# Decoding 64-bit weights: magnitudes on VectorE, signs as 16-bit floats, and three weight loads behind copies of keys and scores

## The chip, the core and the metric

The kernel runs on one core of one Trainium2 chip. The metric is the device time of one execution in microseconds (us); shorter is better. The engines are TensorE (PE: matmuls and transposes; PEld: its weight loads), VectorE (DVE), ScalarE (ACT), GpSimd (POOL) and SyncE (SP, which here issues DMAs). Each works through its own list of instructions in order; semaphores join the lists.

## The reference

Attention over the 32 largest scores of each row, then a feed-forward block with an ELU between two products. Cut to what matters:

```python
# q, k, v: (8, 8, 576, 64) float32
scores = (q @ k.transpose(0, 1, 3, 2)) / sqrt(64)
kth    = the 32nd largest score of each row
attn   = softmax of the scores >= kth (all others -1e9)
x      = (attn @ v), heads side by side      # (4608, 512)
# w_in (512, 2048) and w_out (2048, 512) arrive as float64
h = x @ w_in
g = where(h > 0, h, exp(min(h, 0)) - 1)
out = g @ w_out                              # (4608, 512) float32
```

## The kernel before

**Weights.** The two weight matrices arrive as 64-bit floats, and no engine computes with these. So the kernel reads them as pairs of 32-bit words and makes 32-bit floats of them itself: 16 tiles of `w_in` and 16 of `w_out`, each of 128 partitions x 512 weights (512 KB as loaded). `load_weight(i)` issues the DMA of tile i into a buffer named `raw` (seven buffers). Then come, for each tile:

- `convert_first`: ScalarE makes the low word into a float whose bits hold the upper mantissa part (L174), writes the sign as an 8-bit float into the top byte of the low word's place (L175, Sign), and takes the absolute value of the high word, read as a 32-bit float (L178, Abs). GpSimd clamps that value (L179).
- `convert_last`: VectorE shifts the clamped word left by 3 (L186), and GpSimd adds the two words as integers into the final `w_in` or `w_out` tile (L187).

All these operations step over 8 bytes from one element to the next, since the high and low words alternate.

**The list of pieces.** `decode` holds 35 pieces; `hook()` takes the next one. Piece i issues the load of tile i+3, does `convert_first(i)` and then `convert_last(i-3)`. Hooks stand in VectorE's selection of the 32 largest scores: behind two of the MAX8 passes of each of the two rows' halves in steps 0 to 7, and behind three of step 8. Three loads (tiles 0 to 2) are issued ahead of all, between the loads of the first queries, keys and values.

**Steps.** A step is one block of 128 queries for a pair of heads. TensorE turns queries and keys by transposes (`transpose_qk`, copied by ScalarE into `kqT`, L264 and L277) and computes scores (L301), ScalarE copies them scaled into `sc` (L309). VectorE finds the 32 largest of each row: four MAX8 passes (L320 and L330 in `select_row` up to step 7; L343 and L355 in `select` from step 8) with three MATCH_REPLACE8 between (L324, L348). GpSimd makes two small operands (L368, L370), ScalarE masks and exponentiates (L371, L372), GpSimd normalises (L382 to L389), TensorE transposes the result (L408, copied at L409) and multiplies by the values (L434, copied at L461).

**Feed-forward.** `ffn_pieces` cuts the feed-forward work into pieces that `feed` spreads between the steps: `hidden` (L506, with ScalarE's two Relus at L516 and L519, the Exp at L521, and VectorE's joining operation at L478) and `project` (L531, output copied by ScalarE at L540, stored by SP). A piece of the first block only goes in when enough weight tiles are decoded.

**Order.** From step 8 on, and for the first keys and scores, the order of each compute engine is the written one (`manual_schedule`). In between, steps 0 to 7, the framework orders the instructions of each engine itself.

Of the kernel before, what the change touches and what calls it, by code (L numbers as in the profile page):

```python
# [8 lines left out]
AF = mybir.ActivationFunctionType  # L9
ALU = mybir.AluOpType  # L10
FP32 = mybir.dt.float32
U32 = mybir.dt.uint32
I32 = mybir.dt.int32
FP8 = mybir.dt.float8e4
PSUM = bass.MemoryType.PSUM

TOP_K = 32
# [2 lines left out]
STEEP = 1.0e30  # L20
HIDDEN = {1: 1.1, 2: 1.85, 3: 2.7}
PROJECT = 3.55


class Tile:
# [56 lines left out]
def kernel(  # L82
# [9 lines left out]
    nc = tc.nc  # L92
# [9 lines left out]
    NF = dff // P  # L102
# [3 lines left out]
    scale = 1.0 / float(D) ** 0.5  # L106
# [33 lines left out]
    raw = {}  # L140

    def weight(i):
        per = dff // WN
        if i < NC * per:
            f, c = divmod(i, NC)
            src = moe_w_in[c * P : (c + 1) * P, 2 * f * WN : 2 * (f + 1) * WN]
            return src, w_in[:, c, f * WN : (f + 1) * WN]
        f = i - NC * per
        return moe_w_out[f * P : (f + 1) * P, :], w_out[:, f, :]

    def load_weight(i):
        t = rawpool.tile([P, 2 * WN], U32, tag="raw", name="raw")
        nc.sync.dma_start(t[:], weight(i)[0])
        raw[i] = t

    def parts(t):
        words = t[:].rearrange("p (n w) -> p n w", w=2)
        signs = t[:].bitcast(FP8).rearrange("p (n w) -> p n w", w=8)
        return words[:, :, 0], words[:, :, 1], signs[:, :, 3]

    def convert_first(i):

        lo, hi, sign = parts(raw[i])
        ef, mf = hi.bitcast(FP32), lo.bitcast(FP32)
        nc.scalar.activation(mf, lo, AF.Copy, scale=2.0**-35, bias=2.0**17)  # L174
        nc.scalar.activation(  # L175
            sign, ef, AF.Sign, scale=2.0**64, bias=1.0, saturate=False
        )
        nc.scalar.activation(ef, ef, AF.Abs, scale=2.0**-62)  # L178
        nc.gpsimd.tensor_scalar(  # L179
            ef, ef, (2.0 - 2.0**-3 - 2.0**-23) * 2.0**-46, 2.0**-77, ALU.min, ALU.max  # L180
        )

    def convert_last(i):
# [21 lines left out]
    def decode_piece(i):  # L205
        if i < 2 * NF:
            if i + 3 < 2 * NF:
                load_weight(i + 3)
            convert_first(i)
        if i > 2:  # L210
            convert_last(i - 3)
            decoded[0] = i - 2

    loaded, kqT, vT = {}, {}, {}

    def load_qk(b, hp, other=nc.sync):

        for name, src in (("k", k), ("q", q)):
            n, queue = (J + 1, nc.sync) if name == "k" else (J, other)
            t = ldpool.tile([P, n, 2, D], FP32, tag=name + "in", name=name + "in")  # L220
            if name == "k":
                last = t
            for hh in range(2):
                queue.dma_start(
                    t[:, 0:J, hh, :],
                    src[b, 2 * hp + hh, 0:JP, :].rearrange("(p j) d -> p j d", j=J),
                )
            queue.dma_start(
                last[0:R, J, :, :] if name == "k" else last[R:P, J, :, :],
                src[b, 2 * hp : 2 * hp + 2, JP:S, :].rearrange("h p d -> p h d"),  # L230
            )
            loaded[b, hp, name] = t

    def load_v(b, hp):

        t = kvpool.tile([P, 2 * J + 2, D], FP32, tag="vT", name="vT")
        for hh in range(2):
            h = 2 * hp + hh
            nc.sync.dma_start(
                t[:, hh * J : (hh + 1) * J, :],  # L240
                v[b, h, 0:JP, :].rearrange("(p j) d -> p j d", j=J),
            )
            mine = slice(hh * R, (hh + 1) * R)
            other = slice((1 - hh) * R, (2 - hh) * R)
            nc.gpsimd.memset(t[other, 2 * J + hh, :], 0.0)
            nc.sync.dma_start(t[mine, 2 * J + hh, :], v[b, h, JP:S, :])
        vT[b, hp] = t
# [234 lines left out]
    def ffn_pieces(blk):  # L482
        n_tok = blk.slots * P
        bank = dm // n_tok
        unit = max(2, bank)

        def hidden(f):
            if f == 0 and blk.number == 0:
                g = early.tile([P, NF, P], FP32, tag="g", name="gT")
                blk.gT = [g[:, 0:NG], g[:, NG:NF]]  # L490
            elif f % NG == 0 and blk.number > 0:
                g = late["g"].tile([P, NG, T], FP32, tag="g", name="gT")
                blk.gT.append(g[:])
            if f % unit == 0:
                if len(gates) > 1:
                    close_gates(upto=gates[0][1])
                if blk.number == 0:
                    n = earlyf.tile([P, 4 * P], FP32, tag="n", name="n")
                else:
                    n = late["f"].tile([P, 2 * T], FP32, tag="n", name="n")  # L500
                blk.n = n[:, 0 : unit * n_tok].rearrange("p (f t) -> p f t", f=unit)
            if f % bank == 0:
                ps = ps_f.tile([P, dm], FP32, tag="f", name="hps")
                blk.h = ps[:, 0 : bank * n_tok].rearrange("p (f t) -> p f t", f=bank)
            for i in range(NC):
                nc.tensor.matmul(  # L506
                    blk.h[:, f % bank, :],
                    w_in[:, i, f * P : (f + 1) * P],
                    blk.xT[:, i, 0:n_tok],
                    start=(i == 0),  # L510
                    stop=(i == NC - 1),
                )
            g, end = blk.gT[f // NG], f % NG + 1
            if end % bank == 0:
                n0 = f % unit + 1 - bank
                nc.scalar.activation(  # L516
                    blk.n[:, n0 : n0 + bank, :], blk.h, AF.Relu, scale=-1.0
                )
                nc.scalar.activation(g[:, end - bank : end, 0:n_tok], blk.h, AF.Relu)  # L519
            if end % unit == 0:  # L520
                nc.scalar.activation(blk.n, blk.n, AF.Exp, scale=-1.0)  # L521
                dst = g[:, end - unit : end, 0:n_tok]
                gates.append((place[0], (blk.number, f + 1 - unit), dst, blk.n))

        def project(s, part):
            close_gates(upto=(blk.number, (part + 1) * NF // 4 - 1))
            if part == 0:
                blk.o = ps_f.tile([P, dm], FP32, tag="f", name="ops")
            step = NF // 4
            for f in range(part * step, (part + 1) * step):  # L530
                nc.tensor.matmul(  # L531
                    blk.o[:],
                    blk.gT[f // NG][:, f % NG, s * P : (s + 1) * P],
                    w_out[:, f, :],
                    start=(f == 0),
                    stop=(f == NF - 1),
                )
            if part == 3:
                o = opool.tile([P, dm], FP32, tag="osb", name="osb")
                nc.scalar.copy(o[:], blk.o[:])  # L540
                for t in blk.tiles[s]:
                    p0 = t.cols.start - s * P
                    nc.sync.dma_start(out[t.rows, :], o[p0 : p0 + t.ql, :])

        part = HIDDEN[blk.slots]
        behind = 2 * NF if blk.number else 0
        return [
            (part, max(behind, NC * (f // 4 + 1)), lambda f=f: hidden(f))
            for f in range(NF)
        ] + [  # L550
            (PROJECT, max(behind, NF + (part + 1) * NF // 4),
             lambda s=s, part=part: project(s, part))
            for s in range(blk.slots)
            for part in range(4)
        ]

    ffn = []
    steps, first, due = [], {}, []
    blocks, tight = [], 2 * NHP
    for b in range(B):  # L560
        if b % 2 == 0:
# [5 lines left out]
            for part in division:  # L567
                blk = Block(len(blocks), len(part))
# [4 lines left out]
        for qt in range(J + 1):  # L573
# [8 lines left out]
            t = Tile(b, qt, rows, blk, slice(c0, c0 + n))  # L582
# [6 lines left out]
        for qts in order:  # L589
# [3 lines left out]
            for qt in qts:  # L593
                n = len(steps)
# [3 lines left out]
    for blk in sorted(blocks, key=lambda x: x.ready):  # L598
        due.append((blk.ready, total))
        total += NF * HIDDEN[blk.slots] + 4 * blk.slots * PROJECT  # L600

# [32 lines left out]
    E = mybir.EngineType  # L634
    engines = {E.PE, E.Activation, E.DVE, E.Pool}
    load_qk(0, 0, nc.scalar)
    load_weight(0)
    load_qk(0, 1)
    load_weight(1)
    load_v(0, 0)  # L640
    load_weight(2)
    with tc.manual_schedule(engines=engines):
        for hp in range(2):
            start_qk(0, hp)
            turn_qk(True)
            scores(steps[hp])
    load_qk(0, 2)
    load_qk(0, 3)
    for hp in range(1, NHP):
        load_v(0, hp)  # L650
    decode += [lambda i=i: decode_piece(i) for i in range(2 * NF + 3)]
    at(0, start_qk, 0, 2)
    at(1, start_qk, 0, 3)
# [93 lines left out]
```

## Time and profile before

| | us |
|---|---|
| median of 3 runs (1667.3 to 1669.78) | 1667.61 |
| profiled execution | 1667.86 |
| its span, first to last instruction | 1666.1 |
| busy PE / DVE / ACT / POOL | 1598.7 / 1495.4 / 1164.9 / 630.4 |
| chain that ended last: PE / DVE / ACT | 68% / 21% / 8% of the span |
| decoding: ScalarE L174, L175, L178 busy up to 180 us | 20.9, 40.9, 21.0 |
| decoding: last shift on VectorE (L186) starts | 148.1 |
| mean TensorE clock granted | 0.972 of full |

Busy times of different engines overlap. "The chain that ended last" goes back from the last instruction, at each step to what released it. A tile of 64-bit weights took 5.1 (`w_in`) and 3.9 us (`w_out`) from issue to landing in the median.

### The profile page before, as it was taken

The numbers are of one execution on the slowest core, as the hardware profiler recorded it, in microseconds if no ns is written. First come the engines' busy times: TensorE is split into PE (matmuls) and PEld (weight loads), VectorE is DVE, ScalarE is ACT, GpSimd is POOL, SyncE is SP. The second block draws the span as 40 slices with busy tenths as digits, with TensorE's granted clock in tenths as the row PEclk, the third lists the DMA queues.
The fourth block names the chain that finished last, engine by engine and source line by source line (L and its number), as shares of the span: only waits on it lengthen the run. The fifth ranks groups of instructions, "written<-read, shape, count | busy, mean of one in ns | idle before, by whom it ended". The sixth has DMA issues, their size and how long they took to land.

```text
span 1666.1 us, 26020 instructions
## 1 busy us (share of the span) xinstructions
PE 1598.7 (96%) x8560; PEld 1037.1 (62%) x8560; DVE 1495.4 (90%) x3044; ACT 1164.9 (70%) x2345; POOL 630.4 (38%) x1719
## 2 busy tenths in 40 slices
PE   5588999999999999999999999999999999999999
PEld 3365777657574767656566676755557575755565
DVE  5887999999999999999999999999999999998500
ACT  6997777668686767678667685868758585857521
POOL 2775444333334334333334333333333343332200
PEclk9568999999999999999999999999999999999999
DMA  7540111001100110011100111001200100000000
GB/s 212 169 145 7 23 48 31 7 15 44 48 1 7 44 42 22 1 28 37 42 14 1 49 29 35 1 14 43 50 13 1 28 15 29 7 7 7 7 14 13
DMA packets 101126, 56.21 MB, mean 34 GB/s; under 512 B 84096, under 2 KB 92288, under 8 KB 100992
## 3 DMA queue, kind: packets, MB, share of 16 engines
q1 hardware_dynamic: 99792, 54.26, 11.7%
q8 instruction: 68, 1.11, 0.3%
q14 instruction: 66, 0.54, 0.1%
q10 hardware_dynamic: 1200, 0.30, 0.1%
HBM read 45.09 MB, written 9.44 MB: 33 GB/s over the span
## 4 chain that ended last, share of the span: by engine, by line
PE 68%; DVE 21%; ACT 8%; issue 1%; POOL 1%; SPq 0%; DMA 0%; ACTq 0%; DVEq 0%; POOLq 0%
PE ops L531 25%; PE hps L506 21%; DVE wk L348 9%; PE avps L434 8%; DVE m L355 8%; PE scps L301 7%; PE eps L408 5%; DVE m L343 3%; ACT raw L175 1%; PE qkps L271 1%; DVE gT L478 1%; ACT sc L372 1%; ACT sc L371 1%; ACT et L409 1%; ACT raw L174 1%
## 5 line engine op out<-in xcount | busy, mean ns | idle before, releaser
L355 DVE MAX8 m<-wk 128x8 f32<-128x576 f32 x816 | 573.1, 741 | 0.0
L506 PE MATMUL hps<-xT,w_in 128*128 128x256 f32 (+2 forms) x2432 | 547.5, 374 | 0.1
L531 PE MATMUL ops<-w_out,gT 128*128 128x512 f32 x1152 | 523.4, 599 | 0.0
L506 PEld LDWEIGHTS hps<-xT,w_in 128*128 128x128 f32 x2432 | 405.8, 192 | 97.8 <-issue 24.8
L348 DVE MATCH_REPLACE8 wk<-m,wk 128x576 f32<-128x576 f32 x544 | 398.2, 737 | 0.0
L531 PEld LDWEIGHTS ops<-w_out,gT 128*128 128x128 f32 x1152 | 208.8, 190 | 233.5 <-issue 221.5
L382 POOL TENSOR_SCALAR dene<-den 128x2 f32<-128x2 f32 x144 | 36.4, 253 | 778.3 <-ACT sc L372 777.6
L371 ACT ACTIVATE sc<-sc,neg 128x576 f32<-128x576 f32 x288 | 226.3, 786 | 79.5 <-POOL neg L368 79.5
L372 ACT ACTIVATE sc<-sc,gap 128x576 f32<-128x576 f32 x288 | 223.8, 777 | 25.2
L301 PE MATMUL scps<-kqT 64*128 64x288 f32 (+1 forms) x1280 | 204.6, 443 | 27.9 <-ACT sc L309 15.6
L309 ACT ACTIVATE sc<-scps 128x576 f32<-128x576 f32 x288 | 173.6, 658 | 76.8 <-PE scps L301 76.8
L389 POOL TENSOR_SCALAR sc<-sc,rec 128x576 f32<-128x576 f32 x288 | 221.2, 778 | 14.9
L409 ACT COPY et<-eps 128x512 f32<-128x512 f32 x288 | 166.6, 578 | 58.1 <-PE eps L408 58.0
L408 PEld LDWEIGHTS eps<-ident,sc 128*128 128x128 f32 x1152 | 144.8, 145 | 88.0 <-issue 48.3
L348 DVE MATCH_REPLACE8 wk<-m,sc 128x576 f32<-128x576 f32 x272 | 199.1, 737 | 0.0
L434 PE MATMUL avps<-et,vT 128*64 128x256 f32 (+2 forms) x2080 | 193.3, 329 | 3.0 <-ACT et L409 2.7
L408 PE MATMUL eps<-ident,sc 128*128 128x128 f32 x1152 | 177.2, 280 | 19.2 <-POOL sc L389 17.9
L478 DVE SCALAR_TENSOR_TENSOR gT<-n,gT 128x512 f32<-128x512 f32 (+1 forms) x132 | 99.1, 751 | 103.1 <-ACT n L521 103.1
L343 DVE MAX8 m<-sc 128x8 f32<-128x576 f32 x272 | 190.5, 739 | 0.0
L301 PEld LDWEIGHTS scps<-kqT 64*128 64x128 f32 (+1 forms) x1280 | 109.0, 182 | 99.4 <-issue 44.9
L434 PEld LDWEIGHTS avps<-et,vT 128*64 128x64 f32 x2080 | 123.4, 142 | 76.2 <-issue 25.1
L516 ACT ACTIVATE n<-hps 128x512 f32<-128x512 f32 (+1 forms) x156 | 87.7, 562 | 72.6 <-PE hps L506 71.0
(46 smaller groups left out, 1160.3 us busy)
## 6 DMA issues: line engine op xcount, KB each, us to landing
kin<-in_k_dram SPq DMA_DIRECT2D x64, 128.0 KB, 2.9
raw<-in_moe_w_in_dram SPq DMA_DIRECT2D x16, 512.0 KB, 5.1
vT<-in_v_dram SPq DMA_DIRECT2D x64, 128.0 KB, 2.3
raw<-in_moe_w_out_dram SPq DMA_DIRECT2D x16, 512.0 KB, 3.9
out_dram<-osb SPq DMA_DIRECT2D x32, 256.0 KB, 2.3
qin<-in_q_dram SPq DMA_DIRECT2D x62, 128.0 KB, 2.8
kin<-in_k_dram SPq DMA_DIRECT2D x32, 32.0 KB, 2.6
vT<-in_v_dram SPq DMA_DIRECT2D x64, 16.0 KB, 2.2
```

The source lines that it names most:

```text
L301: nc.tensor.matmul(wide[i][rows, half, 0:HS], kq[part, q0 : q0 + u.t.ql], kq[part, k0 : k0 + HS], start=True, stop=True,)
L343: nc.vector.max(found[i], cur[i])
L348: nc.vector.match_replace(wk[i], found[i], cur[i], TAKEN)
L355: nc.vector.max(found[i], cur[i])
L371: nc.scalar.activation(sc, sc, AF.Prelu, bias=neg[:], alpha=STEEP)
L372: nc.scalar.activation(sc, sc, AF.Exp, bias=gap[:], accum_out=u.den[:, i : i + 1])
L389: nc.gpsimd.tensor_scalar(u.sc[:, i, :], u.sc[:, i, :], rec[:, i : i + 1], 1.0, ALU.mult, ALU.mult)
L408: nc.tensor.transpose(ps[:, c * P : (c + 1) * P], sc[:, c0 : c0 + P], ident[:])
L409: nc.scalar.copy(g.et[:, chunks, u.at, :], ps[:, 0 : n * P].rearrange("p (c q) -> p c q", c=n),)
L434: nc.tensor.matmul(ps[i * D : (i + 1) * D, cols], vt[:, 2 * J + i if c == J else i * J + c, :], w, start=(c == 0), stop=(c == J),)
L506: nc.tensor.matmul(blk.h[:, f % bank, :], w_in[:, i, f * P : (f + 1) * P], blk.xT[:, i, 0:n_tok], start=(i == 0), stop=(i == NC - 1),)
L531: nc.tensor.matmul(blk.o[:], blk.gT[f // NG][:, f % NG, s * P : (s + 1) * P], w_out[:, f, :], start=(f == 0), stop=(f == NF - 1),)
```

## The change

The absolute value of the high word leaves ScalarE: a new function `convert_next` clears the sign bit on VectorE (a bitwise AND of the 32-bit words) and then does the clamp on GpSimd, one piece later than `convert_first` of the same tile. The sign is written as a 16-bit float into the upper half of the low word's place. Since Abs also scaled by a power of two and Sign's bytes now mean another exponent, the decoded weights carry a factor of 2^-8 (`WEIGHT`), which the two Relus of the hidden layer and the output copy take out again. The loads of weight tiles 0 to 2 move behind the first keys and scores: GpSimd copies one element of `kqT` (tile 0) or of step 0's scores (tiles 1 and 2) into the buffer, and the DMA waits for that copy. The loads of the third pair of heads and of the first values change places with them.

```diff
-    def load_weight(i):
+    def load_weight(i, wait=None):
         t = rawpool.tile([P, 2 * WN], U32, tag="raw", name="raw")
+        if wait is not None:
+            nc.gpsimd.tensor_copy(t[0:1, 0:1], wait.bitcast(U32))
         nc.sync.dma_start(t[:], weight(i)[0])
...
-        signs = t[:].bitcast(FP8).rearrange("p (n w) -> p n w", w=8)
-        return words[:, :, 0], words[:, :, 1], signs[:, :, 3]
+        signs = t[:].bitcast(FP16).rearrange("p (n w) -> p n w", w=4)
+        return words[:, :, 0], words[:, :, 1], signs[:, :, 1]
...
         lo, hi, sign = parts(raw[i])
-        ef, mf = hi.bitcast(FP32), lo.bitcast(FP32)
-        nc.scalar.activation(mf, lo, AF.Copy, scale=2.0**-35, bias=2.0**17)
         nc.scalar.activation(
-            sign, ef, AF.Sign, scale=2.0**64, bias=1.0, saturate=False
+            lo.bitcast(FP32), lo, AF.Copy, scale=2.0**-35, bias=2.0**17
         )
-        nc.scalar.activation(ef, ef, AF.Abs, scale=2.0**-62)
+        nc.scalar.activation(
+            sign, hi.bitcast(FP32), AF.Sign, scale=2.0**64, bias=1.0
+        )
+
+    def convert_next(i):
+        hi = parts(raw[i])[1]
+        nc.vector.tensor_single_scalar(hi, hi, 0x7FFFFFFF, ALU.bitwise_and)
         nc.gpsimd.tensor_scalar(
-            ef, ef, (2.0 - 2.0**-3 - 2.0**-23) * 2.0**-46, 2.0**-77, ALU.min, ALU.max
+            hi.bitcast(FP32), hi.bitcast(FP32),
+            (2.0 - 2.0**-3 - 2.0**-23) * 2.0**17, 2.0**-14, ALU.min, ALU.max,
         )
...
             convert_first(i)
+        if 0 < i <= 2 * NF:
+            convert_next(i - 1)
         if i > 2:
             convert_last(i - 3)
...
-                    blk.n[:, n0 : n0 + bank, :], blk.h, AF.Relu, scale=-1.0
+                    blk.n[:, n0 : n0 + bank, :], blk.h, AF.Relu, scale=-1.0 / WEIGHT
                 )
-                nc.scalar.activation(g[:, end - bank : end, 0:n_tok], blk.h, AF.Relu)
+                nc.scalar.activation(
+                    g[:, end - bank : end, 0:n_tok], blk.h, AF.Relu, scale=1.0 / WEIGHT
+                )
...
-                nc.scalar.copy(o[:], blk.o[:])
+                nc.scalar.activation(o[:], blk.o[:], AF.Copy, scale=1.0 / WEIGHT)
...
     load_qk(0, 0, nc.scalar)
-    load_weight(0)
     load_qk(0, 1)
-    load_weight(1)
-    load_v(0, 0)
-    load_weight(2)
     with tc.manual_schedule(engines=engines):
         for hp in range(2):
             start_qk(0, hp)
             turn_qk(True)
             scores(steps[hp])
     load_qk(0, 2)
+    load_weight(0, kqT[0, 0][0:1, 0:1])
+    load_v(0, 0)
+    load_weight(1, steps[0].sc[0:1, 0, 0:1])
+    load_weight(2, steps[0].sc[0:1, 0, 0:1])
     load_qk(0, 3)
```

More of the change, by code (lines that the diff above doesn't have):

```diff
@@ L13 @@
 I32 = mybir.dt.int32
-FP8 = mybir.dt.float8e4
+FP16 = mybir.dt.float16
 PSUM = bass.MemoryType.PSUM
@@ L22 @@
 PROJECT = 3.55
+WEIGHT = 2.0**-8
 class Tile:
```

## The prediction

> **What bounds the kernel now.** I read the 40 slices first, then the table by stage, then VectorE's waits in the first stage, then the durations of the decoding operations, and last the start in order of time.
>
> The slices show three engines and the clock granted to TensorE:
>
> ```profile
> DVE  5887999999999999999999999999999999998500
> ACT  6997777668686767678667685868758585857521
> POOL 2775444333334334333334333333333343332200
> PEclk9568999999999999999999999999999999999999
> ```
>
> A slice is 41.7 us. VectorE (DVE) is full from the fifth slice to the 36th; only the first four slices have holes. The same four have the low clock. The table by stage puts numbers to it (busy us of PE, PEld, DVE, ACT, POOL, then clock):
>
> ```profile
> 15.55:150.00 134.45, 97.35 (x465) 69.11 (x465) 105.03 (x219) 121.70 (x209) 84.72 (x148) 0.68 0.45 140
> 52.30:138.20 85.90, 68.04 (x330) 50.43 (x328) 62.17 (x128) 84.17 (x145) 63.99 (x111) 0.62 0.43 134
> 150.00:400.00 250.00, 242.88 (x1723) 175.62 (x1721) 250.00 (x513) 184.15 (x382) 99.30 (x288) 0.99 0.10 26
> 400.00:800.00 400.00, 393.92 (x2094) 253.13 (x2091) 400.00 (x818) 292.61 (x603) 154.00 (x442) 1.00 0.11 27
> 800.00:1666.10 866.10, 859.94 (x4269) 536.10 (x4268) 739.89 (x1496) 558.82 (x1143) 289.19 (x829) 1.00 0.07 19
> ```
>
> From 150 to 800 us VectorE never idles, and after that TensorE idles 6 us in 866. So the later stages have no room of their own, and nothing in them is changed but scale factors. What the change is worth is decided before 150 us, while the weights are decoded, and is then carried to the end: VectorE's whole later list moves by the time at which it leaves that stage. TensorE can follow, for it waits about 13 us in all between 150 and 800 us. Inside the stage it is ScalarE (ACT) that is full: 84.17 of 85.90 us in the steady part. VectorE there is only the second, and it stands idle for 134.45 - 105.03 = 29.4 us. Its waits in 15.55 to 150 us:
>
> ```profile
> DVE raw L186 <- POOL raw L179: 22.8, 18, 4.0
> DVE gT L478 <- ACT n L521: 6.0, 2, 3.4
> DVE m L320 <- ACT sc L309: 3.1, 1, 3.1
> ```
>
> (The third lies at 15.55 us itself, before this sum.) Nearly all is the shift of line 186 waiting for GpSimd's clamp (L179), and the clamp in turn waits for ScalarE's Abs (L178): 32.2 us in the first 150. VectorE is held by ScalarE's backlog through two engines. That is the room which the change can use.
>
> **What it removes from ScalarE.** The decoding operations of one weight tile (minimum/median/maximum ns):
>
> ```profile
> L174 ACT ACTIVATE raw<-raw x32: 649/714/808, 8.5 to 138.8; 128x512 f32<-128x512 uint32 x32
> L175 ACT ACTIVATE raw<-raw x32: 1323/1394/1521, 9.2 to 140.4; 128x512 fp8e4<-128x512 f32 x32
> L178 ACT ACTIVATE raw<-raw x32: 628/707/846, 10.5 to 142.2; 128x512 f32<-128x512 f32 x32
> L179 POOL TENSOR_SCALAR raw<-raw x32: 639/656/939, 11.3 to 143.2; 128x512 f32<-128x512 f32 x32
> L186 DVE TENSOR_SCALAR raw<-raw x32: 411/428/1274, 12.0 to 148.1; 128x512 uint32<-128x512 uint32 x32
> ```
>
> The Abs goes: 32 x 0.707 = 22.6 us. The Sign (L175) takes twice what its neighbours take, on the same 512 elements at the same step of 8 bytes; what it alone has is the 1-byte output. With a 2-byte output no row exists. The bounds are 1.394 (no better than fp8) and 0.71 (as L174 and L178). I take 0.71, as two of the three rows have it, and keep the other end as a rival: 32 x 0.68 = 21.9 us. Together 44.5 us off ScalarE. In the steady part 22 weights are decoded, so its 84.2 us fall by 22 x (0.707 + 0.683) = 30.6 to 53.6 us.
>
> The Trainium skill ("ScalarE: Activation LUTs", *What ACT_TABLE_LOAD costs*) lets an ACTIVATE run at one element per cycle for fp32 and bf16 alike, 186 ns + 0.833 ns per element with immediate operands: an estimate of 0.61 us for the new Sign, 3 us less over all weights than I take. It doesn't speak of 1-byte outputs, where this trace has 1.394 us.
>
> **What it adds on VectorE.** 32 ANDs, same shape, type and step as the shift of L186, whose mean in the stage is 0.474 us: 15.2 us. Bounds: 32 x 0.411 = 13.2 us, and 32 x 1.274 = 40.8 us if every one met what the slowest shift met:
>
> ```profile
> 59.57 1.04 POOL L187 TENSOR_TENSOR w_in<-raw 128x512 int32<-128x512 int32 x1
> 59.62 1.27 DVE L186 TENSOR_SCALAR raw<-raw 128x512 uint32<-128x512 uint32 x1
> ```
>
> GpSimd's add started 0.05 us earlier, and the shift took 0.85 us more than its median. The median itself says that this is rare today; I take the mean, which has such cases in it.
>
> This is the rule that speaks against the change: the Trainium skill ("SBUF — State Buffer", *SBUF: two separate sides*) has VectorE's two-port operations and GpSimd share a port pair under an exclusive lock, whoever starts first. If all new ANDs lost that race the sum would be worse by 25.6 us, a clear loss; the 428 ns median is against that.
>
> The AND must wait for the Sign (which reads what it overwrites), and GpSimd's clamp must wait for the AND. Queued behind a waiting AND on VectorE is the whole selection (L320 to L355), so such a wait costs its full length. In program order the AND of weight i-1 is one hook behind its Sign, where before the first VectorE operation of a weight was three hooks behind. But up to step 8 the order isn't the written one (the first conversions ran before the copies of keys that are written ahead of them), so operations may be placed where their inputs are expected.
>
> **The balance of the stage.** VectorE's busy time from its first MAX8 to 150 us becomes 105.0 + 15.2 = 120.2 us. With idle time I, and the start S earlier, the gain is 134.45 + S - 120.2 - I = 14.2 + S - I. Now I is 29.4. What stays of it: where two shifts go in a row the second waits about 0.55 us for the second clamp, eight times, 4.4 us, and ScalarE has no part in that. New: two Signs end 0.6 us apart on ScalarE and an AND takes 0.43, so 0.2 us for each of 16 pairs, 3 us. The 6.0 us of L478 came from ScalarE's queue; I leave 2. So I = 9.4; its ends are 2 (only what L478 leaves) and 29.4 (VectorE waits as long as ever, for other partners).
>
> **The start.** In order of time:
>
> ```profile
> 11.10 0.30 ACT L264 COPY kqT<-scps 128x192 f32<-128x192 f32 x1
> ...
> 14.79 1.26 ACT L309 ACTIVATE sc<-scps 128x576 f32<-128x576 f32 x2
> ...
> 15.55 1.42 DVE L320 MAX8 m<-sc 128x8 f32<-128x576 f32 x2 [3.14 <-ACT sc L309]
> ```
>
> TensorE had the last transpose for these copies ready at 8.54 us. ScalarE was at the three conversions of weight 0 from 8.50 to 11.19. If these can't come first any more, the key copies start when the transposes are ready, 2.6 us earlier; as the first of them could start before the last transpose ends, up to 3.2. I take S = 3.0, bounds 0 (something else takes the place: the key loads were on the chain up to 8.44 us as well) and 3.5.
>
> The three new GpSimd copies of one element cost 0.1 to 0.26 us each (the smallest memsets and L368), while GpSimd idled 9.6 us before its first clamp: nothing. Behind them on GpSimd wait only memsets for values and clamps that need these weights. Behind the waiting transfers on SP stand the values of the first heads, and the third and fourth pairs' keys: load_qk(0, 2) now goes ahead of weight 0, the fourth pair waits for the copy of scores, about 12.4 us, and was issued at 17.15 so far. Each weight load costs SP 0.6 us. Weight 0 is issued after the third pair's loads (3.3 to 4.9 us of issue behind 8.5 us), so at 12 to 13, and lands 4.5 to 5.4 us later, as the first two did: 17 to 18. The first hook now falls at 21.8 us, 3 us earlier at 18.8. It fits by 1 us; the slowest of these loads took 10 us, and then up to 4 us of S are gone.
>
> **Nothing.** The scales in L516, L519 and L540: L516 already has a scale and takes 562 ns. The output copy (586 ns) becomes an ACTIVATE; only the last of 36 lies at the end, at most 0.13 us by L174's 714. GpSimd's clamp has other constants, same operation; the integer add is the same.
>
> **Sum.** Gain 14.2 + 3.0 - 9.4 = 7.8 us. The profiled execution took 1667.86 us with a span of 1666.1, and is 0.25 above the median of 1667.61; I take it from the median: 1659.8, said as 1660.
>
> **The rivals.**
> First, the good end: with ScalarE a third empty every wait goes except those 2 us, and the TensorE gap of 12.4 us (39.4 to 51.8 us), behind which the clock fell to 0.50, closes. For it: the idle time is nearly all of ScalarE's making. Against: the pairs. Gain 14.2 + 3 - 2 = 15.2, so 1652.4.
> Second, slower: VectorE and GpSimd play into each other. A shift stands right behind an AND, GpSimd has just begun the clamp that the AND released, and VectorE is held for one clamp, 0.656 us, per weight: 21.0 us, I = 30.4, 13.2 us lost, 1680.8. The change is a loss from 0.24 us per weight on (7.8 / 32). For it: L187 and L186 above, and GpSimd, with 64.0 us busy plus some 0.08 us between 111 instructions, 73 us, would have to fit into a steady part of about 79, in which the ANDs can hold it in turn by 22 x 0.43 = 9.5. Against: today the shift and GpSimd overlap without harm in the median.
> Third, the 16-bit Sign is as slow as the fp8 one. ScalarE still loses 22.6 us and is no longer full (68.6 of 79), but half of its backlog stays: I = 9.4 + 6, gain 1.8, no change that counts; 1665.8.
>
> **How the numbers follow.** Two measurements of this kernel can be told apart from about 0.2%, 3.3 us. The forecast (I from 5 to 14) has 0.47, the good end 0.15, the ping-pong 0.25, the slow Sign 0.13. So faster 0.62, same 0.13, slower 0.25. The range from 1649 to 1674 holds the first, the third and nearly all of the good end, and from the ping-pong the milder part (up to 0.45 us per weight); about 0.18 is left out above and 0.02 below. The forecast's own range is 1655 to 1665.
>
> **What would show it.** In the profile after: no L178 row, and the Sign at about 0.71 us; ScalarE at 7 tenths or less in the first four slices; VectorE's first MAX8 near 12.5 us; AND at 0.43 to 0.47 us; VectorE's idle time up to the end of decoding about 9 us; the last shift near 140 in place of 148.1 us, and the same distance at the end. Wrong if the Sign stays at 1.39, if VectorE's waits for the clamp or the Sign add up to over 17 us, or if the stage is left earlier and the end isn't.

## The result: 1676.38 us, slower

The changed kernel takes 1676.38 us in the median of four runs (1675.34 to 1678.09), the kernel before 1667.46: a ratio of 1.0051, 95% interval 1.0039 to 1.0063. The profiled execution took 1675.54 us with a span of 1673.7, 7.7 us and 7.6 us more than before. 1660 was predicted.

The lines have moved: Sign L175 is now L179, the new AND is L185, the clamp L179 is L186, the shift L186 is L194, the add L187 is L195; L330 and L340 are the MAX8 passes, L319 the copy of scores, L399 the normalising, L418 and L419 the transposes behind it and their copy, L444 and L471 the product with the values and its copy.

The slices of the changed kernel:

```profile
DVE  5879999999999999999999999999998999998500
ACT  6976786668676777767668685858758585857521
POOL 3766434433433333433333333433333343332200
PEclk7577999999999999999999999999999999999999
```

ScalarE is down from 9 to 7 tenths in the third slice and from 7 to 6 in the fourth, and VectorE is up from 7 to 9 in the fourth (and down from 8 to 7 in the third). That alone looks like what was meant. The table by stage says more (busy us of PE, PEld, DVE, ACT, POOL, then clock); its first stretch goes from VectorE's first MAX8 to the end of the last shift. First the kernel before, then the changed one, whose second line is the stretch behind:

```profile
15.55:148.54 132.99, 95.89 (x457) 68.43 (x457) 103.57 (x216) 121.70 (x209) 83.45 (x146) 0.68 0.45 141
12.18:155.22 143.04, 91.64 (x456) 65.06 (x457) 118.27 (x249) 111.63 (x182) 87.11 (x148) 0.67 0.46 142
155.22:400.00 244.78, 236.71 (x1689) 170.57 (x1688) 244.78 (x502) 176.59 (x366) 99.75 (x284) 1.00 0.10 25
```

So the start came 3.4 us earlier, VectorE's busy time grew by 14.7 us, and its idle time fell only from 29.4 to 24.8 us: -3.4 + 14.7 - 4.6 = 6.7 us more at the end of decoding. From there on VectorE is full in both kernels, and 7.6 us arrive at the end. TensorE's granted clock in the stage is 0.67 against 0.68, so it isn't the difference. Where the idle time comes from now (waits of VectorE up to 180 us: total, times, longest):

```profile
DVE raw L185 <- ACT raw L179: 18.7, 13, 6.2
DVE m L330 <- ACT sc L319: 12.2, 1, 12.2
DVE raw L194 <- POOL raw L186: 5.8, 4, 4.4
```

The second is the start itself. The wait of the shift for the clamp, 22.8 us before, has shrunk to 5.8; in its place the new AND waits for ScalarE's Sign, 18.7 us. The wait of L478, 6.0 us before, is gone. The Sign is one cause (minimum/median/maximum ns):

```profile
L176 ACT ACTIVATE raw<-raw x32: 647/670/744, 19.5 to 137.9; 128x512 f32<-128x512 uint32 x32
L179 ACT ACTIVATE raw<-raw x32: 1322/1350/1452, 20.8 to 138.6; 128x512 f16<-128x512 f32 x32
L185 DVE TENSOR_SCALAR raw<-raw x32: 400/428/1085, 22.2 to 147.6; 128x512 uint32<-128x512 uint32 x32
L186 POOL TENSOR_SCALAR raw<-raw x32: 642/657/1047, 22.8 to 149.2; 128x512 f32<-128x512 f32 x32
L194 DVE TENSOR_SCALAR raw<-raw x32: 402/419/1281, 25.5 to 154.8; 128x512 uint32<-128x512 uint32 x32
```

With a 16-bit output it takes 1.350 us, against 1.394 with an 8-bit one: nothing was gained by the format. The longest wait shows the second cause. In order of time:

```profile
86.82 1.11 PE L418 MATMUL eps<-ident,sc 128*128 128x128 f32 x4 [4.62 <-POOL sc L399]
...
87.97 0.59 ACT L419 COPY et<-eps 128x512 f32<-128x512 f32 x1 [3.16 <-PE eps L418]
...
94.50 0.27 ACT L471 COPY xT<-avps 128x128 f32<-128x128 f32 x1 [0.96 <-PE avps L444]
94.66 1.22 ACT L176 ACTIVATE raw<-raw 128x512 f32<-128x512 uint32 x2
...
95.78 2.48 ACT L179 ACTIVATE raw<-raw 128x512 f16<-128x512 f32 x2
97.14 0.43 DVE L185 TENSOR_SCALAR raw<-raw 128x512 uint32<-128x512 uint32 x1 [6.18 <-ACT raw L179]
```

TensorE waits for GpSimd's normalising; ScalarE, in order, waits for TensorE's transposes and then for its products before it comes to the Sign, and VectorE stands at the AND for 6.18 us. From the end of the Sign before (84.80 us) to the end of this one (97.14) ScalarE works for 6.16 of 12.34 us; it isn't full there, half of the time it waits. VectorE, the bound engine, has been tied to the softmax of an earlier step through three queues. The same shows in the whole stage: ScalarE stands idle there for 31.4 us (143.04 - 111.63), against 11.3 before (132.99 - 121.70), and its waits for TensorE's transposes have grown from 1.9 to 12.7 us. Before (L408 and L409), then after:

```profile
ACT et L409 <- PE eps L408: 1.7, 2, 1.0
ACT et L409 <- PE scps L408: 0.2, 1, 0.2
ACT et L419 <- PE eps L418: 9.2, 9, 3.2
ACT et L419 <- PE scps L418: 3.5, 5, 1.1
```

These idle times alone don't say which engine began to be late, for the engines wait for each other in a ring; the experiments have to.

### The profile page after: what moved, and what is told of

Same layout as the page of the kernel before. It is cut to its first block, busy times and chain, and to the rows that moved or that the text cites. A ratio compares the mean times of both kernels' runs of the same rounds, so it can differ in the third digit from the quotient of the medians.

```text
span 1673.7 us, 26037 instructions
## 1 busy us (share of the span) xinstructions
PE 1594.1 (95%) x8560; PEld 1033.3 (62%) x8560; DVE 1510.6 (90%) x3076; ACT 1150.0 (69%) x2313; POOL 633.2 (38%) x1722
## 4 chain that ended last, share of the span: by engine, by line
PE 66%; DVE 24%; ACT 5%; issue 2%; POOL 2%; DMA 1%; SPq 0%; ACTq 0%; POOLq 0%; DVEq 0%
PE ops L543 23%; PE hps L516 22%; DVE wk L358 10%; DVE m L365 8%; PE avps L444 8%; PE scps L311 7%; PE eps L418 5%; DVE m L353 3%; DVE gT L488 1%; PE qkps L281 1%; ACT sc L382 1%; ACT sc L381 1%; PE scps L418 1%; ACT raw L179 1%; ACT raw L176 1%
## 5 line engine op out<-in xcount | busy, mean ns | idle before, releaser
L399 POOL TENSOR_SCALAR sc<-sc,rec 128x576 f32<-128x576 f32 x288 | 222.8, 784 | 15.0
L319 ACT ACTIVATE sc<-scps 128x576 f32<-128x576 f32 x288 | 173.5, 658 | 78.7 <-PE scps L311 78.6
L418 PE MATMUL eps<-ident,sc 128*128 128x128 f32 x1152 | 177.2, 279 | 36.1 <-POOL sc L399 34.9
L419 ACT COPY et<-eps 128x512 f32<-128x512 f32 x288 | 166.0, 577 | 65.0 <-PE eps L418 64.7
L418 PEld LDWEIGHTS eps<-ident,sc 128*128 128x128 f32 x1152 | 144.3, 144 | 105.9 <-issue 47.5
L444 PE MATMUL avps<-et,vT 128*64 128x256 f32 (+2 forms) x2080 | 191.9, 327 | 4.1 <-ACT et L419 3.9
L444 PEld LDWEIGHTS avps<-et,vT 128*64 128x64 f32 x2080 | 123.0, 142 | 77.0 <-issue 24.5
```

Of the source, the lines that this page charges most:

```text
L319: nc.scalar.activation(u.sc[:, i, :].rearrange("p (a s) -> p a s", a=2), wide[i][:, :, 0:HS], AF.Copy, scale=scale,)
L399: nc.gpsimd.tensor_scalar(u.sc[:, i, :], u.sc[:, i, :], rec[:, i : i + 1], 1.0, ALU.mult, ALU.mult)
L418: nc.tensor.transpose(ps[:, c * P : (c + 1) * P], sc[:, c0 : c0 + P], ident[:])
L444: nc.tensor.matmul(ps[i * D : (i + 1) * D, cols], vt[:, 2 * J + i if c == J else i * J + c, :], w, start=(c == 0), stop=(c == J),)
```

## The experiments

The first set divides the change and tests the Sign.

**The loads alone** (e1): the kernel before, with the diff's parts in `load_weight` and in the order of loads only.

> The kernel before with only the three weight loads moved behind the copies of keys and scores. Theory (the start is gained, the stage is lost by the decoding): the first MAX8 near 12.2 us as in the changed kernel, 3.4 us earlier than before, and all of it reaches the end: 3 us less than before, about 1664.3. Rival (late weights do the harm): the first conversions come later, VectorE waits for them, and the time is at or above before, 1667.5 to 1672.

1667.34 us, ratio 0.9994 (0.9985 to 1.0003): no difference. The first MAX8 is at 12.23 us, the last shift ends at 147.81, 0.7 us earlier than before. Of the 3.3 us won, 2.6 are lost inside the stage. The shifts of the first three tiles show where (VectorE in order of time; in this kernel the shift is L188, the clamp L181):

```profile
23.36 0.43 DVE L188 TENSOR_SCALAR raw<-raw 128x512 uint32<-128x512 uint32 x1 [1.39 <-POOL raw L181]
26.10 0.43 DVE L188 TENSOR_SCALAR raw<-raw 128x512 uint32<-128x512 uint32 x1 [1.64 <-POOL raw L181]
30.33 0.43 DVE L188 TENSOR_SCALAR raw<-raw 128x512 uint32<-128x512 uint32 x1 [0.30 <-POOL raw L181]
```

Before, the first shift ran at 11.96 us, while VectorE had nothing else to do, and the next two waited for nothing. Now the tiles come later and the bound engine waits 3.3 us for them. The rival held but for 0.2 us of its range: the start is won, and nearly all of it is paid back.

**The decoding alone** (e2): the changed kernel with the three loads in their old places.

> The changed kernel with the three weight loads where they were before. Theory (the decoding loses some 10 us in the stage, whatever the loads do): 3 to 4 us more than the changed kernel, about 1679.5, 12 more than before. Rival (late weights do the harm): less than the changed kernel, 1667 to 1672.

1672.89 us, ratio 1.003 (1.0019 to 1.0041): slower than before by 5 us, but 3.5 us faster than the whole change, where my theory had it 3 to 4 us slower; the rival had the direction, and its range missed by 0.9 us. The loss is the decoding's, and with it the moved loads cost something more: the idle time in the stage is 19.0 us (15.68 to 152.43 us, 117.77 busy) against 24.8. The two parts aren't additive.

**The Sign with a 32-bit output** (e3).

```diff
-            sign, hi.bitcast(FP32), AF.Sign, scale=2.0**64, bias=1.0
+            lo.bitcast(FP32), hi.bitcast(FP32), AF.Sign, scale=2.0**64, bias=1.0
```

> The changed kernel with the Sign written as a 32-bit float over the whole low word (the three lowest bits of the decoded weights are lost, WEIGHT is 2^-1); every instruction stands at the same place in its engine's order. Theory (it is the 1.36 us of the Sign that VectorE waits for): Sign 0.67 us, VectorE's idle time between its first MAX8 and the last shift falls from 24.8 to about 9 us, the time by about 15 to 1661. Rival (VectorE and GpSimd hold each other up, or the AND stands too near behind its Sign): the Sign is faster, but the idle time stays above 18 us and the time above 1669. Second rival (the Sign is slow in itself, not by its output type): its row stays at 1.3 us and nothing changes.

1668.94 us, ratio 1.0004 (0.9994 to 1.0013), 7.4 us less than the changed kernel, half of what I expected and 0.1 us short of the rival's 1669. The Sign now takes 0.665 us, so it is the output that was slow, not the function. VectorE's idle time falls from 24.8 to 17.6 us. Its waits up to 160 us:

```profile
DVE m L330 <- ACT sc L319: 12.2, 1, 12.2
DVE raw L185 <- ACT raw L179: 11.0, 8, 3.8
DVE raw L194 <- POOL raw L186: 6.3, 3, 4.3
```

A wait of 3.75 us at 92.22 us is what is left of the 6.18 us above, and the 4.4 us wait for a clamp is still 4.3. So the slow Sign is about half of the 15 us that I looked for; the other half is still there with a fast Sign, as the rival had it.

**Probes of ScalarE's and VectorE's outputs** (e4), behind the last computation.

> The changed kernel with probes behind its last computation, on 128 x 256 elements of a scratch tile, six of each: ScalarE's Sign to 32-bit output; Copy to 16-bit float output at steps of 8, 4 and 2 bytes; Copy to bfloat16 at 8; Sign to 16-bit float at 8; and VectorE's (x AND 0x8000) OR 0x3C00 on 16-bit words at 8 bytes. If a 2-byte output as such is slow: all 16-bit rows some 0.7 us, the 32-bit Sign 0.4. If it is the step of 8 bytes with a 2-byte element: only the rows at 8 (and perhaps 4) are slow, the contiguous one 0.4. If it is the function: both Sign rows are slow, the copies not.

Groups by line; the last column but one is the busy time and mean ns. L737 is Sign to 32 bits at steps of 8 bytes (three of its six lie before this window); L739, L741 Copy to 16-bit float and bfloat16 at 8; L743 Copy to 16 bits at 4, L745 at 2 bytes; L747 Sign to 16 bits at 8; L752 VectorE on 16-bit words at 8:

```profile
L739 ACT ACTIVATE pout<-probe 128x256 f16<-128x256 f32 x6 | 4.6, 769 | 0.2
L741 ACT ACTIVATE pout<-probe 128x256 bf16<-128x256 f32 x6 | 4.6, 768 | 0.2
L747 ACT ACTIVATE pout<-probe 128x256 f16<-128x256 f32 x6 | 4.6, 768 | 0.2
L743 ACT ACTIVATE pout<-probe 128x256 f16<-128x256 f32 x6 | 2.9, 488 | 0.2
L752 DVE TENSOR_SCALAR pout<-probe 128x256 uint16<-128x256 uint16 x6 | 2.7, 452 | 47.7 <-ACT pout L747 47.5
L745 ACT ACTIVATE pout<-probe 128x256 f16<-128x256 f32 x6 | 2.6, 427 | 0.2
L737 ACT ACTIVATE pout<-probe 128x256 f32<-128x256 f32 x3 | 1.3, 427 | 0.1
```

So neither the function nor the 2-byte type as such makes the Sign slow. A 2-byte element per 8 bytes costs 768 ns for 256 elements, side by side 427, the same as 4-byte elements at the same step of 8. The extra 341 ns are 1.33 ns an element; the Sign in the changed kernel has 685 ns over the 32-bit form for 512, 1.34 ns an element. The 16-bit operation of VectorE takes 452 ns for 256 elements, more than the 428 ns of the AND on 512 words; no experiment makes the signs there.

The second set tests how VectorE is tied to ScalarE's queue.

**AND later** (e5): `convert_next(i - 2)` and `convert_last(i - 4)`, the next load at the end of a piece.

> The changed kernel with the AND and clamp two pieces behind the Sign instead of one, and the shift and add four behind instead of three (36 pieces; the next load is issued at the end of a piece). Theory (the AND stands so near behind its Sign that VectorE inherits every delay of ScalarE's queue): the long waits of VectorE (6.2, 4.4, 2.3, 1.8 us in the changed kernel) shrink to below 2 us each, its idle time in the stage from 24.8 to about 14, the time by 8 to 11, to 1666 to 1668. Rival (the slow Sign sets the pace whatever the distance): within 3 us of the changed kernel, 1673 to 1679.

1669.96 us, ratio 1.001 (1.0 to 1.002), 6.8 us below the changed kernel by the ratios; a little less than expected. The wait of 6.18 us has become 1.41, but others are still up to 3.2 us long (2.95 for a clamp), where all were expected below 2, and the idle time is 20.5 us, not 14. Since the next load moved as well, this isn't the distance alone.

**AND later and Sign as 32 bits** (e6).

> The kernel of e5_and_later with the Sign written as a 32-bit float as in e3_sign_as_f32 (the three lowest bits of the decoded weights are lost); its order is that of e5_and_later on every engine. Theory (distance and the slow Sign together are the missing time): idle time of VectorE in the stage at most 9 us, against 17.6 in e3_sign_as_f32, the time 1658 to 1662, as the prediction had it. Rival (the distance doesn't matter): as e3_sign_as_f32, 1667 to 1670.

1663.78 us, ratio 0.9971 (0.996 to 0.9982): 5.5 us less than with the 32-bit Sign alone by the ratios (0.0033 of 1668), and the first version with the AND that is faster than the kernel before. It falls short of the expected 1662 by 2: the idle time is 14.2 us, not 9. The two causes act side by side: the Sign is worth 7.8 us by the ratios at the near distance (1.0051 to 1.0004) and 6.5 at the far one (1.001 to 0.9971).

**No AND, Abs on ScalarE as before, Sign as 32 bits, loads moved** (e7).

> The kernel of e1_loads_only (Abs on ScalarE, no AND on VectorE) with the Sign written as a 32-bit float over the low word (the three lowest bits of the decoded weights are lost; scales adjusted, WEIGHT is 2^-1). Theory (ScalarE's 22 us of slow Sign are what the stage can give, and the AND's 15 us on VectorE give them back): VectorE's busy time in the stage stays at 104 to 105 us, its idle time falls from 31 to 10 to 16, the time by 15 to 20, to 1647 to 1653. Rival (VectorE waits for the chain through GpSimd and TensorE, not for the Sign): idle above 24, 1660 or more.

1656.03 us, ratio 0.9927 (0.991 to 0.9944): 11.3 us less than the loads alone, where 15 to 20 were expected. VectorE's busy time in the stage is 103.3 us and its idle time 21.5, down from 31.1. This undoes the AND and keeps ScalarE busy with Abs, and is faster than any version with the AND. The 21.5 us that are left, where 10 to 16 were expected, are not the slow output's: the Sign takes 0.692 us here.

**AND left out** (e8).

```diff
-        nc.vector.tensor_single_scalar(hi, hi, 0x7FFFFFFF, ALU.bitwise_and)
```

> The changed kernel without the AND (the magnitudes keep their sign bit, so the clamp turns every negative weight into the smallest magnitude; everything else is there). Theory: VectorE loses 16.4 us of busy time and its direct wait for the Sign (18.7 us), but the shift still waits for a clamp that waits for the Sign: idle 15 to 25, the time 1676 - 16 - 0 to 9 = 1651 to 1660. Rival (the AND costs little, it fills time in which VectorE would wait anyway): 1668 or more.

1658.97 us, ratio 0.9941 (0.9922 to 0.9961), 17.4 us below the changed kernel (medians) or 18.3 (ratios). The stage:

```profile
12.33:139.36 127.03, 95.94 (x467) 67.96 (x468) 103.11 (x217) 109.83 (x183) 84.52 (x148) 0.69 0.52 159
```

VectorE's idle time is 127.0 - 103.1 = 23.9 us, against 24.8 with the AND. So the AND's 15 us of work come off in full, and the waits hardly change: they go from the AND to the shift, one engine further on. The AND filled no idle time; it stood beside it.

This run set beside e1 (same loads, Abs on ScalarE, no AND) shows the other side of the exchange: without the Abs, and with the clamp one piece later, VectorE's idle time falls from 31.1 to 23.9 us and the time by 8.4, from 1667.34 to 1658.97. So what left ScalarE was worth some 8 us, and the AND that paid for it some 17.

**A faster version**: e7 without ScalarE's conversion of the low word (e9), and the same with the loads where they were before (e10).

> The kernel of e7_abs_on_act_f32 without ScalarE's conversion of the low word, which the 32-bit Sign overwrites anyway: two operations of ScalarE per weight tile instead of three (the three lowest bits of the decoded weights are lost, as in e7). Theory (ScalarE's queue still sets what is left of VectorE's waits, 21 us): 22 us less on ScalarE, VectorE's idle time from 21 to 12 to 16, the time from 1656 to 1647 to 1651. Rival (what is left comes from GpSimd and TensorE): 1654 to 1657.

> The kernel of e9_no_low_word with the three weight loads where they were before. Theory (the start gained by the moved loads is lost again, because three tiles that were decoded while VectorE had nothing to do are now waited for in the stage): within 2 us of e9_no_low_word. Rival (with ScalarE relieved, the 3.4 us of the start stay): 3 to 4 us slower than e9_no_low_word.

1651.41 us, ratio 0.9895 (0.9878 to 0.9911), and 1654.54 us, ratio 0.9915 (0.99 to 0.993). The first is the best kernel of this study, 17.7 us below the kernel before; like e3, e6 and e7 it gives up the three lowest bits of the weights. Its stage:

```profile
12.10:133.83 121.73, 91.59 (x467) 65.40 (x468) 103.34 (x217) 92.22 (x183) 86.47 (x148) 0.72 0.54 167
```

ScalarE is relieved by another 15 us, and the idle time falls only from 21.5 to 18.4, where 12 to 16 were expected: little of it was still ScalarE's load. The time came within 0.4 us of the theory's range all the same. In e10 the rival held: the medians are 3.1 us apart, and each of its four runs (1654.22 us and more) is slower than each of e9's (1652.98 and less). So by these runs the moved loads do help once ScalarE is relieved. The profiled executions show only a part of it: their spans are 1.7 us apart (1651.1 and 1652.8), and the stage ends 0.8 us earlier (133.83 against 134.63) for a start 3.0 us earlier.

## Why the prediction was wrong

The frame held. With the measured start and idle time the prediction's own formula gives 14.2 + 3.4 - 24.8 = -7.2 us; the profiled executions differ by -7.7. The stage decided, and the later stages carried what it left. The step that failed is the idle time I, said to be 9.4 us and found at 24.8. Of its three terms, the new wait of the AND behind its Sign was said to be 3 us and measured 18.7 (13 waits, the longest 6.18); the shift's wait for the clamp was said to be 4.4 and measured 5.8; L478 was said to be 2 and measured nothing. Both of the signs of being wrong that bear on it came: the Sign stayed near 1.39, and the waits for Sign and clamp add up to 24.5 us, over 17. Behind it stand three misreadings:

- **The Sign**, 0.71 us taken, 1.350 measured. The third rival had this as a possibility, at 0.13, and its condition came true; its time of 1665.8 didn't. The choice between fp8's row and the 32-bit rows went by counting rows; the step of 8 bytes was named and dismissed, since the 32-bit rows have it too, but in the probes it costs extra only with 2-byte elements. What the slow Sign costs was sized about right: 6 us in the third rival, 7.2 us of idle time in e3. But with the fast Sign the idle time is still 17.6 us, not 9.4, and the time only level with the kernel before, so a fast Sign alone would not have made the forecast true.
- **Where the new wait binds.** I had seen that the AND is one hook behind its Sign, and set this aside because the framework might place it well. VectorE's wait for the clamp, and through it for the Abs, was read as ScalarE's load. But an engine in order is late also when it waits, and with less of its own to do (111.6 us busy in the stage against 121.7) ScalarE was late behind TensorE and GpSimd; the trace shows it for the longest wait. Moving the AND back is worth 5.5 to 6.8 us (e5, e6, with the load moved too). How much of the idle time was load shows without any AND: e9 takes some 47 us off ScalarE against e1 (32 x (2.84 - 1.36), the medians of its operations on a tile), and VectorE's idle time falls by 12.7 us, from 31.1 to 18.4. The forecast had 20 us of idle time for 44.5 us off ScalarE, with an AND to wait for as well.
- **The start**: S was measured at 3.4 (3.0 said), but in e1 and in the changed kernel it isn't kept. Before, the first tile was shifted at 11.96 us, ahead of VectorE's first MAX8, and the second was begun; the next two shifts, at 25.87 and 26.93 us, waited for nothing. (It wasn't three tiles that were done ahead, as I wrote for e10.) Moved behind the scores the first tiles are waited for: 3.3 us in e1 and 3.4 in the changed kernel (2.29 and 1.12 us at 22.16 and 24.38 us). The prediction had the first of the moved loads issued at 12 to 13 us and landed at 17 to 18; it was issued at 14.6, and ScalarE began on it at 19.5. I had a condition for that ("It fits by 1 us"), and took the good side of it for the sum. Of the 5.8 us by which the changed kernel's idle time exceeds that of e2, 2.4 are left without an explanation.

Of the 15.4 us between the forecast's idle time and the measured one the fast Sign takes away 7.2 (e3) and the distance another 3.4 (e6). The 4.8 us that remain have causes that no run here takes apart; of the 14.2 us of idle time in e6 the trace puts 7.2 down to the wait for the clamp on GpSimd and 6.9 to the Sign.

**What was right**: the AND's price (15.2 us said; 14.7 us of busy time more, and 16 to 18 us of time by e8, whose span is 16.2 us shorter), which is a real cost on the bound engine and hidden by nothing. The Abs left ScalarE. The scale factors cost next to nothing: the output copy takes 598 ns in place of 586.

**The ping-pong rival** had the right sign (13.2 us lost by it, 8.9 measured), and a mechanism that the rows don't bear out. It named the lock between VectorE's two-port operations and GpSimd (the Trainium skill, "SBUF — State Buffer", *SBUF: two separate sides*). The rows leave it a small term at most: the AND's mean in the stage is 0.512 us and the shift's 0.489, against 0.474 for the shift before, 32 x 0.038 + 32 x 0.015 = 1.7 us together, not 21. On GpSimd the clamp got shorter (a mean of 685 ns in the stage, 727 before) and the normalising longer (818 against 751 ns, 14 times, some 1 us).

The other page of the prediction (the Trainium skill, "ScalarE: Activation LUTs", *What ACT_TABLE_LOAD costs*) has one element per cycle for fp32 and bf16 alike. The probes come near it for 32-bit floats (427 ns for 256 elements, against an estimate of 399 from the page's formula) and differ for bfloat16 at steps of 8 bytes (768 ns): the measurement decides.

## What to carry to other kernels

Work that moves from a full engine to the bound one can cost its whole duration there, as the AND did, and then pays only if the waits it removes are longer; they are if they were waits for the first engine's load, and not for what that engine waits for; leave the moved operation out once (as e8 does) to see which they are. Before you count an idle time as won, follow it past the engine that is named: a queue in order is late for whatever stands ahead in it. And a transfer that is moved out of the way of the start takes with it the work that was done there for nothing: in e1 this cost nearly all of what the start won, in e9 it didn't.

## What the hardware showed

In the probes ScalarE wrote 16-bit floats side by side in 427 ns for 128 x 256, as fast as 4-byte elements at steps of 8 bytes (427); at steps of 4 bytes they took 488, and at steps of 8 bytes 768. Those 768 ns came for 16-bit float and bfloat16, and for Copy and Sign alike. In the decoding the 8-bit output at steps of 8 bytes took 1.394 us for 128 x 512, about as long as the 16-bit one (1.350).
